# Chunk 0 of a three-stage kernel: first weights read as unsplit float32, one order for chunks 0 and 1, eight weight tiles split in the last chunk

## The chip, the core and the metric

The kernel runs on one core of one Trainium2 chip. The metric is device time in microseconds (us) of one execution. The kernel before took 981.0 us, the median of three runs (980.6 to 983.09). The engines are TensorE (PE, with its weight loads as PEld), VectorE (DVE), ScalarE (ACT), GpSimd (POOL) and the DMA queue of SyncE (SP).

## The reference

Three stages follow one another: a linear attention over 8 heads of width 64, a gated feed-forward layer (SwiGLU after an RMS norm), and a second feed-forward layer with a rational function in place of the gate.

```python
q_s = softmax(q, axis=-1); k_s = softmax(k, axis=2)
kv = np.einsum('bhsd,bhse->bhde', k_s, v)
x = np.einsum('bhsd,bhde->bhse', q_s, kv)            # as 2304 tokens x 512
xn = x / sqrt(mean(x * x) + 1e-06) * rms_g
y = (silu(xn @ w_gate) * (xn @ w_val)) @ w_out       # d_ff 1536
h = y @ w_in                                         # second layer, d_ff 2048
P = a[0] + a[1]*h + a[2]*h*h + a[3]*h*h*h
Q = 1.0 + abs(b[0])*abs(h) + abs(b[1])*h*h
out = (P / (Q + 1e-06)) @ w_out2
```

The weight matrices are float64. q, k, v and the output are float32.

## The kernel before, in words

The 2304 tokens are worked through in six chunks (c = 0 to 5) of T = 384 tokens. For each chunk the kernel makes the attention output x (four tiles of 128x384), its RMS norm, and then goes over f = 0 to 11, the twelve column blocks of the first layer: a projection g with the gate weights, a projection v with the value weights, the product u = silu(g)*v, and y += u times a tile of w_out. y goes to DRAM. When all six chunks are done, a last phase goes over the six chunks again with the sixteen blocks of the second layer (h, the rational function, o).

**Weights.** Each weight tile is 128x512 float64 in DRAM (512 KB). The first layer has 36 (numbered in order of need: g0, v0 are 0 and 1, then for each f the tiles g, v and the o of the block before), the second layer has 32. A tile is loaded raw and turned into float32 by four steps, `conv_exp` and `conv_low` (usually ACT), `conv_sign` and `conv_join` (DVE). Then it is split in two parts of the fast matmul format (fp32r): `conv_hi` (a rounding copy, ACT or DVE) and `conv_lo` (the rest, a subtraction on POOL). x and u are split in the same way, and a product is three fp32r matmuls (`mm3`, lines 649 to 651): high times high, high times low, low times high. One projection is 4 x 3 = 12 matmuls of 128x384.

**Order.** All engine queues are in program order. In chunk 0 the program order is the table `ORDER` (lines 23 to 44), a list of named events. `l7` loads tile 7, `ce7 cl7 cs7 cj7 ch7 co7` are its six steps, `g3 v3 s3 p3 ph3 pl3 y3` the steps of block 3 (projections, silu, product, high and low part of u, output projection), `a...` and `b...` are the attention of chunks 0 and 1, `arp arn arb` the RMS norm of chunk 0, `wN` are N dummy matmuls. Tables `LOW_ACT`, `HI_DVE` and `ALT` choose the engine of single steps. Chunk 0 thus holds the conversion and split of all 36 tiles, its own attention and that of chunk 1. Its first two blocks are projected before the norm is known (`g<-xr`), so g, u and x are multiplied by the norm afterwards (`scale_g`, `scale_u`, `x_mult`).

Chunks 1 to 5 run in a plain loop (line 1038, `u_step`). While chunks 1 to 4 are projected, `schedule(c + 1)` makes the next chunk's attention, and `stage` (line 247) loads, converts, splits and writes to DRAM ("parks") eight second-layer tiles per chunk, 32 in all; it uses the slots of tiles 0 to 3, which are therefore parked first and fetched again. Chunk 5 has no attention to make and only fetches parked tiles (`fetch_to`).

```python
 208         nc.gpsimd.tensor_tensor(
 209             out=t[:, 1, :], in0=tmps.pop(i).bitcast(F32), in1=t[:, 0, :], op=ALU.subtract
 210         )
1060                 tick = lambda part: None if last else stage(c, f, part)
```

Of the kernel before, what the change touches and what calls it, by code (L numbers as in the profile page):

```python
# [19 lines left out]
LOW_ACT = (0, 1, 3, 4, 5, 6, 7, 8, 9, 11, 13, 16, 17, 19, 20, 21, 22, 23, 24, 25, 27, 31, 32, 33)  # L20
HI_DVE = (0, 3, 11, 12, 13, 14, 15, 16, 18, 19, 20, 23, 24, 27, 28, 29, 33, 34)
ALT = ('bqd0', 'bqn0', 'bqn1', 'xm0', 'xl0', 'xm1', 'xl1', 'bxl0', 'bxl1', 'bxl3', 'gr0', 'pl0', 'pl1', 'pl2', 'pl5', 'pl9', 'pl11')
ORDER = """
w9 lk0 akm0 alq akt0 w4 lk1 akx0 lv0 lv1 aqm aks0 w1 akm1 akt1 w2 aqd1 akd0 akx1 aks1 w2 aqd0 ake0 akz0 aqe l0
akv0 w2 akd1 aqs lg ake1 akz1 ce0 l1 cl0 cl1 akn0 aqn0 cs0 ce1 akv1 axq0 cj0 axq1 aqn1 axq2 l2 akn1 cs1 cl2
axq3 blk axc0 l3 axx0 l4 axc1 axc2 axx1 axx2 ce2 ch0 axc3 axs0 axs1 bkz0 l5 co0 axh0 axs2 l6 axh1 l7 axx3 axh3
cj1 blv0 axs3 ch1 cs2 axh2 add1 bkm0 add2 axl0 cj2 ce3 l8 bkt0 add3 l9 bkx0 xw0 ce4 ch2 cl3 co1 axl1 ce5 axl3
bks0 arp axl2 xw1 g0 co2 bkd0 arn l10 cs3 cj3 xw2 ce6 v0 cl6 l11 ch3 l12 cl4 bke0 silu arb ars cl5 l13 cs4 g1
cj4 gm0 xw3 ch4 ce8 cs5 l14 co3 ce7 xm3 xm0 s0 xh0 cj5 gr0 xm2 p0 gm1 co4 cl7 xm1 ch5 cs6 ph0 xl0 l15 xh1 pl0
cj6 bkv0 co5 v1 l16 xl1 xh2 s1 xh3 cl9 y0 cs7 ce9 ch6 gr1 xl2 xl3 l17 cl8 cl10 l18 cl12 ce11 cj7 ch7 cs8 cl11  # L30
l19 p1 ph1 co6 bkz1 ce10 cs9 l20 co7 cj8 pl1 ch8 cj9 ce12 cs10 co8 ch9 cl13 bkn0 cj10 ch10 g2 v2 l21 cs11 ce14
cl14 co9 ce13 cj11 cs12 ch11 l22 co10 co11 s2 l23 cs14 y1 l24 cj12 g3 lc ch12 p2 cs13 cl16 ce17 cl17 l25 ph2
s3 cl15 ce16 ce19 v3 cj13 p3 g4 ce15 cl18 co12 ch13 cj14 v4 blq pl2 cl20 ph3 ch14 co13 s4 pl3 ce20 cs16 cs17
cs15 cj15 ch15 y2 ce18 l26 p4 co14 cj16 co15 ch16 l27 cl21 cj17 cs18 cl19 y3 ce22 g5 ce21 l28 cs19 l29 co16
cs20 ch17 cl22 ph4 ce23 cj18 const v5 ch18 ce26 co17 l30 cj19 s5 co18 cl23 ch19 cs22 cs21 cj20 g6 l31 bqm pl4
ch20 ce24 v6 co19 cl25 p5 cl26 ce25 cl27 co20 blr ph5 cl24 bqd1 y4 s6 cj21 bqd0 g7 cj22 ch21 co21 ch22 cs23
ce28 cs24 co22 p6 v7 l32 pl5 bqe cj23 ch23 ph6 co23 cj24 cl28 l33 pl6 ch24 s7 ce33 cl31 ce27 co24 y5 cs25 bkm1
cj25 g8 ce31 ce29 p7 ch25 bqs s8 cs26 y6 cl32 l34 blv1 ph7 cj26 co25 cl29 bqn0 ch26 bqn1 cs27 v8 pl7 p8 bkt1
ce32 cs32 cs28 bkx1 y7 cl34 bxq0 bks1 cj27 ce34 l35 ph8 bkd1 co26 ch27 cl30 ce30 g9 bxq1 cs29 bxc0 cj28 pl8
co27 cj29 bke1 cl33 bxx0 ch28 s9 ch29 bxc1 co28 bkv1 bxq2 bxs0 cs30 cj30 bxo0 ce35 bxx1 bkn1 ch30 bxo1 co29  # L40
bxc2 co30 cs31 v9 bxs1 cs33 bxq3 cj31 ch31 bxa1 bxx2 cl35 g10 p9 bxc3 ph9 bxs2 pl9 cj32 bxa2 bxx3 bxs3 cs34
co31 cs35 ch32 bxo2 v10 s10 bxa3 brp cj33 co32 bxo3 y8 p10 ch33 cj34 co33 brn ph10 g11 ch34 cj35 brb ch35 bxm0
bxm3 bxm1 s11 co34 v11 y9 pl10 bxl0 bxm2 p11 bxl3 bxl1 bxl2 y10 co35 ph11 pl11
# [4 lines left out]
def kernel(  # L48
# [66 lines left out]
    W1 = {}  # L115
    W2 = {}
# [5 lines left out]
    done = {"load": 0}  # L122
# [48 lines left out]
    def conv_low(i):  # L171
        w, r = words(i)
        if i in LOW_ACT:
            nc.scalar.activation(w[:, :, 0], w[:, :, 0], AF.Copy, scale=7.49 * 2.0 ** -32)
            return
        nc.vector.tensor_scalar(
            out=w[:, :, 0], in0=w[:, :, 0], scalar1=2.0 ** -29, scalar2=7.0,
            op0=ALU.mult, op1=ALU.min,
        )
# [82 lines left out]

    up = ctx.enter_context(tc.tile_pool(name="up", bufs=1))
# [232 lines left out]

    def rms_pe(c, rp):
# [64 lines left out]
    def x_scale(c, p, rp):  # L562
# [101 lines left out]
    def emit_y():  # L664
        c, f, uh, ul = pend_y.pop(0)
        w = W1["o", f]
        if f == 0:
            acc_y[c] = [pa.tile([P, 512], F32, tag=f"a{m}", name=f"y_{c}_{m}") for m in range(KD)]
        for m in range(KD):
            ws = slice(m * P, (m + 1) * P)  # L670
            mm3(acc_y[c][m][:, :T], w[:, 0, ws], w[:, 1, ws], uh, ul, f == 0, f == F1 - 1)
        if f == F1 - 1:
            t = big_tile(F32, ytag(c), f"y_{c}").rearrange("p (c n) -> p c n", n=T)
            for m, o in enumerate(acc_y.pop(c)):
                if c == NCH - 1 and m % 2:
# [116 lines left out]
    def o_pe(s):  # L792
# [5 lines left out]
        for t in range(TT):  # L798
# [25 lines left out]
    with tc.manual_schedule():  # L824

        k1 = bp.tile([P, 2, SC, D], F32, tag=big[3], name="k_0_1")
        v1 = bp.tile([P, 2, SC, VW], F32, tag=big[4], name="v_0_1")
# [3 lines left out]
        nc.vector.memset(cb[:, 1:2], -64.0 * LN2)  # L831
        for t in (vt0, v1):
# [3 lines left out]
        def warm(n):  # L836
            t = ps("warm")
# [12 lines left out]
        def engine(name, one, two):  # L850
            return two if name in ALT else one

        def bank(name, fn, pool=None, tag=None):
            def matmuls():
                t = ps(name) if pool is None else pool.tile([P, 512], F32, tag=tag, name=name)
# [22 lines left out]
        for n in range(1, 17):  # L878
# [233 lines left out]
```

## Time and profile before

| | before |
|---|---|
| runs | 980.6, 981.0, 983.09 us (median 981.0) |
| profiled execution, its own time | 980.75 us |
| its span, first to last instruction | 979.0 us |
| busy PE / PEld / DVE / ACT / POOL | 929.8 / 871.1 / 683.6 / 579.8 / 231.6 us |
| share of the span | 95 / 89 / 70 / 59 / 24 % |
| DMA moved | 108.92 MB, mean 111 GB/s |

The page gives busy time by engine, then the span in 40 slices of some 24.5 us with the busy share of each engine in tenths, and TensorE's granted clock in the same tenths. Matmuls overlap one another in the records, so the pace of TensorE is read from the distance between two starts, not from the length of one record.

### The profile page before, as it was taken

Reading aid. Unit: us, or ns where it says so; the run is one execution under the profiler, and the core shown is the slowest. Engines: PE = TensorE matmul, PEld = TensorE weight load, DVE = VectorE, ACT = ScalarE, POOL = GpSimd, SP = SyncE. Lnnn points to the kernel's source line nnn. Section 1 sums busy time; section 2 is a strip of 40 time slices with the busy share of each in tenths; the row PEclk is TensorE's granted clock in tenths of the full one; section 3 lists DMA queues with packets and bytes.
Section 4 is the critical chain, followed back from the end, with each engine's and each line's share of the span. In section 5 each row is a group of like instructions: output and inputs, shape, how many; then the busy total and the mean of one; then the engine's idle time right before and its main releaser. Section 6 shows DMA issues by size and latency. Waiting matters only on the chain.

```text
span 979.0 us, 14267 instructions
## 1 busy us (share of the span) xinstructions
PE 929.8 (95%) x5408; PEld 871.1 (89%) x5408; DVE 683.6 (70%) x1160; ACT 579.8 (59%) x1069; POOL 231.6 (24%) x208
## 2 busy tenths in 40 slices
PE   7777779999999999999999999999999999999998
PEld 6666679999989998999999999999999999999997
DVE  7999995667666657756730058877777777777776
ACT  3655653553354254336331268888788888878876
POOL 3855533000000000000002213423324224234222
PEclk8899989999999999999999999999999999999999
DMA  9996003346454726344448730010010010100000
GB/s 260 349 308 201 1 1 108 130 172 192 141 158 167 202 89 194 132 153 168 172 175 274 251 117 1 1 65 1 1 65 1 27 40 1 65 1 1 33 1 32
DMA packets 69588, 108.92 MB, mean 111 GB/s; under 512 B 22672, under 2 KB 49296, under 8 KB 69520
## 3 DMA queue, kind: packets, MB, share of 16 engines
q1 hardware_dynamic: 69520, 108.02, 34.6%
q8 instruction: 42, 0.69, 0.3%
q14 instruction: 26, 0.21, 0.1%
HBM read 79.70 MB, written 28.31 MB: 110 GB/s over the span
## 4 chain that ended last, share of the span: by engine, by line
PE 81%; DVE 11%; SPq 3%; DMA 2%; issue 2%; ACT 1%; DVEq 0%
PE h L651 7%; PE h L649 7%; PE o L804 7%; PE o L803 7%; PE h L650 7%; PE o L802 7%; PE vv L649 4%; PE vv L650 4%; PE vv L651 4%; PE y L651 4%; PE y L649 4%; PE y L650 4%; PE g L649 4%; PE g L651 4%; PE g L650 4%; DVE raw L183 3%
## 5 line engine op out<-in xcount | busy, mean ns | idle before, releaser
L790 POOL TENSOR_TENSOR gl<-t,gh 128x384 fp32r<-128x384 f32 x94 | 104.5, 1112 | 253.4 <-ACT gh L788 223.1
L651 PE MATMUL h<-y,wf 128*128 128x384 f32 x384 | 129.5, 337 | 0.0
L649 PE MATMUL h<-y,wf 128*128 128x384 f32 x384 | 129.3, 337 | 0.0
L650 PE MATMUL h<-y,wf 128*128 128x384 f32 x384 | 128.9, 336 | 0.0
L763 DVE SCALAR_TENSOR_TENSOR A<-S,absb,A 128x384 f32<-128x384 f32 x96 | 61.6, 642 | 92.9 <-ACT A L753 92.9
L687 ACT ACTIVATE uh<-u 128x384 fp32r<-128x384 f32 x72 | 37.8, 524 | 132.3 <-DVE u L696 113.2
L804 PE MATMUL o<-wf,gl 128*128 128x512 f32 x288 | 114.1, 396 | 0.0
L803 PE MATMUL o<-wf,gh 128*128 128x512 f32 x288 | 113.7, 395 | 0.0
L802 PE MATMUL o<-wf,gh 128*128 128x512 f32 x288 | 112.0, 389 | 0.0
L650 PE MATMUL y<-ul,w 128*128 128x384 f32 x288 | 98.0, 340 | 5.9 <-DVE ul L692 4.3
L649 PE MATMUL y<-uh,w 128*128 128x384 f32 x288 | 99.2, 344 | 4.5 <-ACT uh L687 4.5
L692 POOL TENSOR_TENSOR ul<-u,uh 128x384 fp32r<-128x384 f32 x18 | 19.2, 1068 | 329.5 <-ACT uh L687 329.4
L651 PE MATMUL y<-uh,w 128*128 128x384 f32 x288 | 96.9, 337 | 0.0
L649 PE MATMUL g<-x,w 128*128 128x384 f32 x248 | 86.6, 349 | 3.1 <-DVE w L200 3.1
L651 PE MATMUL g<-x,w 128*128 128x384 f32 x248 | 84.8, 342 | 3.4 <-POOL w L208 3.4
L696 DVE TENSOR_TENSOR u<-u,vv 128x384 f32<-128x384 f32 x60 | 33.0, 551 | 78.5 <-PE vv L651 78.5
L650 PE MATMUL g<-x,w 128*128 128x384 f32 x248 | 84.3, 340 | 0.0
L183 DVE TENSOR_SCALAR raw<-raw 128x512 uint16<-128x512 uint16 x68 | 63.5, 962 | 25.1 <-ACT raw L230 24.6
L703 ACT ACTIVATE u<-g 128x384 f32<-128x384 f32 x60 | 29.3, 488 | 82.1 <-PE g L651 82.1
L649 PEld LDWEIGHTS h<-y,wf 128*128 128x128 f32 x384 | 72.2, 188 | 4.1
L650 PEld LDWEIGHTS h<-y,wf 128*128 128x128 f32 x384 | 72.1, 188 | 4.0
L649 PE MATMUL vv<-x,w 128*128 128x384 f32 x208 | 70.5, 339 | 1.7 <-DVE u L696 1.7
(205 smaller groups left out, 2377.7 us busy)
## 6 DMA issues: line engine op xcount, KB each, us to landing
wf<-sd SPq DMA_DIRECT2D x48, 512.0 KB, 4.4
sd<-ws SPq DMA_DIRECT2D x32, 512.0 KB, 3.0
raw<-in_moe_w_out_dram SPq DMA_DIRECT2D x28, 512.0 KB, 5.0
raw<-in_moe_w_in_dram SPq DMA_DIRECT2D x16, 512.0 KB, 4.6
raw<-in_moe_w_gate_dram SPq DMA_DIRECT2D x12, 512.0 KB, 9.3
raw<-in_moe_w_val_dram SPq DMA_DIRECT2D x12, 512.0 KB, 10.4
k<-in_k_dram SPq DMA_DIRECT2D x8, 576.0 KB, 6.5
v<-in_v_dram SPq DMA_DIRECT2D x16, 288.0 KB, 6.9
```

Of the source, the lines that this page charges most:

```text
L183: nc.vector.tensor_scalar(out=h[:, :, 1], in0=h[:, :, 3], scalar1=0x8000, scalar2=None, op0=ALU.bitwise_and)
L649: nc.tensor.matmul(o, lhsT=lh, rhs=rh, start=start, stop=False)
L650: nc.tensor.matmul(o, lhsT=lh, rhs=rl, start=False, stop=False)
L651: nc.tensor.matmul(o, lhsT=ll, rhs=rh, start=False, stop=stop)
L687: nc.scalar.activation(uh, u, AF.Copy)
L696: nc.vector.tensor_tensor(out=u, in0=u, in1=vv[:, :T], op=ALU.mult)
L703: nc.scalar.activation(u, g[:, :T], AF.Silu)
L763: nc.vector.scalar_tensor_tensor(out=out, in0=in0, scalar=scalar, in1=in1, op0=op0, op1=op1)
L790: eng.tensor_tensor(out=r["gl"], in0=r["t"], in1=r["gh"], op=ALU.subtract)
L802: nc.tensor.matmul(o, lhsT=r["gh"][:, ts], rhs=w[:, 0], start=first, stop=False)
L803: nc.tensor.matmul(o, lhsT=r["gh"][:, ts], rhs=w[:, 1], start=False, stop=False)
L804: nc.tensor.matmul(o, lhsT=r["gl"][:, ts], rhs=w[:, 0], start=False, stop=last)
```

## The change

The diff touches four things.

1. Sixteen tiles (`WHOLE`: g and v of blocks 0 to 3, o of blocks 0 to 7) are joined into float32 tiles that stay in the slots of tiles 28 to 35, two to a slot. In chunk 0 `proj_whole` and `y_whole` multiply them unsplit, as plain float32, with unsplit x and u: one matmul in place of three. They are split as well, for the later chunks.
2. The early projection with x before the norm is gone; chunk 0 waits for its norm.
3. `ORDER` now covers chunks 0 and 1 and the attention of chunk 2 (`d...`); names carry the chunk (`g1_3`). The engine tables are new: 18 of the 36 `conv_lo` run on DVE, 7 of the `conv_low` and 3 of the `conv_hi`; in both chunks the low part of u is made on DVE. The loop starts at chunk 2.
4. Chunk 1 stages no second-layer tiles. The eight that it staged are loaded raw, converted and split in chunk 5 (`last_load`, `stage_last`, `last_split`), and are not parked.

```diff
-LOW_ACT = (0, 1, 3, 4, 5, 6, 7, 8, 9, 11, 13, 16, 17, 19, 20, 21, 22, 23, 24, 25, 27, 31, 32, 33)
+NF, NY = 4, 8
+WHOLE = (0, 1, 2, 3, 4, 5, 6, 7, 8, 9, 10, 13, 16, 19, 22, 25)
+LOW_DVE = (0, 4, 9, 14, 16, 24, 35)
+HI_DVE = (1, 3, 7)
+LO_POOL = (1, 6, 7, 8, 10, 12, 14, 15, 16, 17, 20, 22, 25, 28, 29, 32, 33, 34)
 ORDER = """
-w9 lk0 akm0 alq akt0 w4 lk1 akx0 lv0 lv1 aqm aks0 w1 akm1 akt1 w2 aqd1 akd0 akx1 aks1 w2 aqd0 ake0 akz0 aqe l0
+lg alk0 akz1 bkz1 akz0 bkz0 alq akm0 alk1 w28 akt0 alv1 aqm akx0 akm1 aqd1 w19 aks0 alv0 aqd0 akd0 w10 akt1
...
     def conv_join(i):
-        w, r = words(i)
-        tmps[i] = wp.tile([P, 512], U32, tag="tmp", name=f"tmp_{i}", bufs=2)
...
+        if i in WHOLE:
+            n, h = divmod(WHOLE.index(i), 2)
+            if n not in sh:
+                sh[n] = wp.tile([P, 1024], F32, tag=f"s{N1 - 1 - n}", name=f"whole_{n}")
+            tmps[i] = sh[n][:, 512 * h:512 * h + 512]
+            W1F[order[i][1:]] = tmps[i]
+        else:
+            tmps[i] = wp.tile([P, 512], F32, tag="tmp", name=f"tmp_{i}", bufs=2)
+        join(i, tmps[i].bitcast(U32))
...
     def conv_lo(i):
...
+        eng = nc.gpsimd if i in LO_POOL else nc.vector
+        eng.tensor_tensor(out=lo, in0=tmps.pop(i), in1=hi, op=ALU.subtract)
...
+    def last_load(n):
+        i = N1 + n
...
+    def last_split(n):
...
+        nc.scalar.activation(hi, tmp, AF.Copy)
+        nc.vector.tensor_tensor(out=lo, in0=tmp, in1=hi, op=ALU.subtract)
+
+    def stage_last(f, part):
+        n = f - 2
+        if part == 0 and 0 <= n - 1 < PARK:
+            last_split(n - 1)
+        if part == 1 and 0 <= n < PARK:
+            stage_words(1, n)
+        if part == 2 and 0 <= n < PARK:
+            stage_join(1, n)
...
+    def proj_whole(o, w, x):
+        for kk in range(KD):
+            ws = slice(kk * P, (kk + 1) * P)
+            nc.tensor.matmul(
+                o[:, :T], lhsT=w[:, ws], rhs=x[:, kk, :], start=(kk == 0), stop=(kk == KD - 1)
+            )
...
+    def y_whole(c, f, u):
+        for m, o in enumerate(acc_tiles(c, f)):
+            nc.tensor.matmul(
+                o[:, :T], lhsT=W1F["o", f][:, m * P:(m + 1) * P], rhs=u,
+                start=(f == 0), stop=(f == F1 - 1),
+            )
...
+        def project(c, which, f, t):
+            if c == 0 and f < NF:
+                proj_whole(t, W1F[which, f], st["xs", 0])
+            else:
+                proj(t, W1[which, f], c)
...
-        for c in range(1, NCH):
+        for c in range(2, NCH):
...
-                tick = lambda part: None if last else stage(c, f, part)
+                tick = lambda part: stage_last(f, part) if last else stage(c, f, part)
```

**What moves on DVE after the norm of chunk 0.** The rows below are DVE's queue from the end of the norm to the product of block 0 (`u_0...<-u_0...,v_...`). `raw` rows are conversions of a tile, `tmp` and `whole` are joins, `w` a high or low part, `xs` and `x_0` the normed x and its low part. Before:

```order
L183 TENSOR_SCALAR raw_295<-raw_295 128x512
L190 SCALAR_TENSOR_TENSOR tmp_412<-raw_295 128x512
L200 CAST w_432<-tmp_412 128x512
L183 TENSOR_SCALAR raw_299<-raw_299 128x512
L190 SCALAR_TENSOR_TENSOR tmp_460<-raw_299 128x512
L1004 TENSOR_TENSOR u_0_462<-g_380,rs_441 128x384
L183 TENSOR_SCALAR raw_316<-raw_316 128x512
L955 TENSOR_TENSOR xs_362<-xs_362,rs_441 128x384
L190 SCALAR_TENSOR_TENSOR tmp_479<-raw_316 128x512
L1007 TENSOR_TENSOR u_0_462<-u_0_462,rs_441 128x384
L955 TENSOR_TENSOR xs_362<-xs_362,rs_441 128x384
L1015 TENSOR_TENSOR u_0_462<-u_0_462,v_416 128x384
```

Changed:

```order
L659 TENSOR_TENSOR x_0_509<-xs_373,x_0_508 128x384
L201 SCALAR_TENSOR_TENSOR whole_379<-raw_462 128x512
L195 TENSOR_SCALAR raw_466<-raw_466 128x512
L195 TENSOR_SCALAR raw_377<-raw_377 128x512
L186 TENSOR_SCALAR raw_540<-raw_540 128x512
L195 TENSOR_SCALAR raw_423<-raw_423 128x512
L195 TENSOR_SCALAR raw_540<-raw_540 128x512
L201 SCALAR_TENSOR_TENSOR whole_358<-raw_423 128x512
L201 SCALAR_TENSOR_TENSOR whole_573<-raw_540 128x512
L1072 TENSOR_TENSOR u_0_560<-u_0_560,v_0_547 128x384
```

The scalings of u and the split of the first tiles are gone from this stretch; what stands between the norm and the first product is only conversions up to the join.

**What moves on TensorE at the first blocks.** `g_`, `v_` are the projections, `y_0` to `y_3` the four output tiles, `bkt` belongs to the attention of chunk 1. Before, the first output projection:

```order
L649 MATMUL y_0_560<-uh_0_492,w_465 128x384
L650 MATMUL y_0_560<-ul_0_498,w_465 128x384
L651 MATMUL y_0_560<-uh_0_492,w_465 128x384
L649 MATMUL y_1_561<-uh_0_492,w_465 128x384
L650 MATMUL y_1_561<-ul_0_498,w_465 128x384
```

Changed, from the first projection of chunk 0 on:

```order
L748 MATMUL g_0_532<-xs_373,whole_383 128x384 x4
L748 MATMUL v_0_547<-xs_373,whole_383 128x384 x4
L748 MATMUL g_1_575<-xs_373,whole_358 128x384 x4
L748 MATMUL v_1_592<-xs_373,whole_358 128x384 x4
L764 MATMUL y_0_607<-u_0_560,whole_573 128x384
L764 MATMUL y_1_608<-u_0_560,whole_573 128x384
L764 MATMUL y_2_609<-u_0_560,whole_573 128x384
L764 MATMUL y_3_610<-u_0_560,whole_573 128x384
L417 MATMUL bkt_628<-ident,m_0_586 128x128
L748 MATMUL g_2_633<-xs_373,whole_573 128x384 x4
```

Three matmuls have become one, which takes u itself and no longer its two parts.

**What moves on DVE at the end of chunk 0.** The rows end or begin around the product of block 11 (`u_11`). Before, the last rows of chunk 0 and the first of chunk 1:

```order
L200 CAST w_1403<-tmp_1371 128x512
L190 SCALAR_TENSOR_TENSOR tmp_1405<-raw_1151 128x512
L564 SCALAR_TENSOR_TENSOR xs_1248<-xs_1248,gk,brb 128x384 x4
L1015 TENSOR_TENSOR u_11_1419<-u_11_1419,v_1422 128x384
L573 TENSOR_TENSOR x_1_1413<-xs_1248,x_1_1412 128x384
L692 TENSOR_TENSOR ul_11_1471<-u_11_1419,uh_11_1469 128x384
L696 TENSOR_TENSOR u_0_1496<-u_0_1496,vv_0_1498 128x384
```

Changed (`w_861`, `w_388` are the low parts of tiles 2 and 3, `raw_1156`, `raw_1400` the conversions of tiles 35 and 34, `mq` and `q` the attention of chunk 2):

```order
L231 TENSOR_TENSOR w_861<-whole_358,w_861 128x512
L201 SCALAR_TENSOR_TENSOR tmp_1378<-raw_1055 128x512
L1072 TENSOR_TENSOR u_11_1376<-u_11_1376,v_11_1321 128x384
L231 TENSOR_TENSOR w_388<-whole_358,w_388 128x512
L231 TENSOR_TENSOR w_1383<-tmp_1378,w_1383 128x512
L477 TENSOR_REDUCE mq_1402<-q_1352 128x24
L802 TENSOR_TENSOR ul_10_1418<-u_10_1289,uh_10_1373 128x384
L485 TENSOR_TENSOR q_1352<-q_1352,mq_1402 128x768
L186 TENSOR_SCALAR raw_1156<-raw_1156 128x512
L802 TENSOR_TENSOR ul_11_1439<-u_11_1376,uh_11_1433 128x384
L195 TENSOR_SCALAR raw_1156<-raw_1156 128x512
L1072 TENSOR_TENSOR u_0_1441<-u_0_1441,v_0_1385 128x384
```

Before, every tile was converted when the last product of chunk 0 stood in the queue; now splits of early tiles and the conversion of tiles 34 and 35 stand behind it, among the first products of chunk 1.

## Rows read from the trace of the kernel before

**Rows 1.** The page: busy time, and 40 slices of the span (busy tenths).

```profile
PE 929.8 (95%) x5408; PEld 871.1 (89%) x5408; DVE 683.6 (70%) x1160; ACT 579.8 (59%) x1069; POOL 231.6 (24%) x208
PE   7777779999999999999999999999999999999998
```

**Rows 2.** Busy time by window: length, engines with instruction counts, clock, DMA share, GB/s.

```profile
33.00:158.60 125.60, 98.37 (x607) 89.51 (x608) 121.49 (x174) 67.77 (x120) 72.28 (x53) 0.92 0.49 152
158.60:238.70 80.10, 80.10 (x459) 78.60 (x458) 50.13 (x81) 36.57 (x67) 1.94 (x5) 1.00 0.45 152
520.00:540.00 20.00, 20.00 (x117) 20.00 (x116) 1.66 (x3) 3.96 (x8) 4.78 (x5) 1.00 0.79 252
```

**Rows 3.** TensorE in order of time: start, length, line, tiles, idle time before.

```profile
39.84 0.81 PE L553 MATMUL arb<-acc,ones 128*128 128x384 f32 x2
40.19 0.63 PE L649 MATMUL g<-xr,w 128*128 128x384 f32 x1
40.66 0.34 PE L650 MATMUL g<-xr,w 128*128 128x384 f32 x1
...
158.65 0.33 PE L649 MATMUL g<-x,w 128*128 128x384 f32 x1
158.82 0.33 PE L650 MATMUL g<-x,w 128*128 128x384 f32 x1
...
238.19 0.33 PE L649 MATMUL g<-x,wf 128*128 128x384 f32 x1
```

**Rows 4.** DVE in order of time, the same columns, up to the end of chunk 0.

```profile
23.34 0.76 DVE L183 TENSOR_SCALAR raw<-raw 128x512 uint16<-128x512 uint16 x1
23.87 0.47 DVE L176 TENSOR_SCALAR raw<-raw 128x512 uint32<-128x512 uint32 x1
...
24.58 0.69 DVE L190 SCALAR_TENSOR_TENSOR tmp<-raw 128x512 uint32<-128x512 uint32 x1
25.18 1.82 DVE L183 TENSOR_SCALAR raw<-raw 128x512 uint16<-128x512 uint16 x1
...
34.13 0.15 DVE L508 TENSOR_SCALAR rw<-arp 128x3 f32<-128x3 f32 x1
...
50.41 0.54 DVE L1004 TENSOR_TENSOR u<-g,rs 128x384 f32<-128x384 f32 x1
50.88 0.73 DVE L183 TENSOR_SCALAR raw<-raw 128x512 uint16<-128x512 uint16 x1
...
155.23 0.55 DVE L1015 TENSOR_TENSOR u<-u,v 128x384 f32<-128x384 f32 x1 [0.45 <-ACT u L1012]
```

**Rows 5.** Groups by line, operation and shape, 0 to 160 us: busy, mean ns, idle before.

```profile
L183 DVE TENSOR_SCALAR raw<-raw 128x512 uint16<-128x512 uint16 x36 | 39.5, 1150 | 0.1
L190 DVE SCALAR_TENSOR_TENSOR tmp<-raw 128x512 uint32<-128x512 uint32 x36 | 36.3, 1012 | 0.9 <-DVE raw L183 0.5
L345 DVE TENSOR_REDUCE m<-k 128x128 f32<-128x1152 f32 x4 | 8.6, 2155 | 3.6 <-DMA k<-in_k_dram 3.6
L428 DVE TENSOR_REDUCE sumq<-q 128x24 f32<-128x1536 f32 x2 | 3.5, 1752 | 0.0
L208 POOL TENSOR_TENSOR w<-tmp,w 128x512 fp32r<-128x512 f32 x36 | 55.0, 1531 | 52.7 <-DVE w L200 21.3 <-ACT w L202 20.2 <-issue 4.2
L385 PE MATMUL bkv<-v,k 64*64 64x65 f32 x144 | 4.6, 219 | 0.0
```

**Rows 6.** The same view from 160 us to the end.

```profile
L183 DVE TENSOR_SCALAR raw<-raw 128x512 uint16<-128x512 uint16 x32 | 24.0, 749 | 25.0 <-ACT raw L230 24.6
L190 DVE SCALAR_TENSOR_TENSOR tmp<-raw 128x512 uint32<-128x512 uint32 x32 | 22.2, 693 | 1.2
L242 DVE TENSOR_TENSOR ws<-tmp,ws 128x512 fp32r<-128x512 f32 x32 | 22.1, 691 | 20.2 <-ACT ws L241 20.2
```

**Rows 7.** What TensorE waited for, 33 to 158.6 us: total us, times, longest.

```profile
PE y L649 <- ACT uh L687: 4.5, 3, 3.8
PE y L650 <- DVE ul L692: 4.3, 4, 1.5
```

More of the change, by code (lines that the diff above doesn't have):

```diff
@@ L494, in x_out, with rms_pe_0 @@
             x_add(c, p, nc.vector)
+    def rms_pe_0(p, rp):
+        for t in range(TT):
+            nc.tensor.matmul(
+                rp[:, TT * p + t:TT * p + t + 1], lhsT=sh["sq_0"][:, p, t * P:(t + 1) * P],
+                rhs=ones[:, 0:1], start=True, stop=True,
+            )
     def rms_pe(c, rp):
@@ L848, in put, with bank @@
             ev[name] = lambda: fn(*args)
[L850 to L853 removed]
+        def bank(name, fn):
             def matmuls():
[L855 removed]
+                t = ps(name)
                 banks[name] = t
@@ new lines @@
+                put(f"{pre}xh{p}", x_high, c, p)
+                put(f"{pre}xl{p}", x_rest, c, p, nc.vector)
+            if c == 0:
+                bank("arp0", lambda t: rms_pe_0(0, t))
+                for p in range(1, NP):
+                    reader(f"arp{p}", "arp0", lambda t, p=p: rms_pe_0(p, t))
+                reader("arn", "arp0", rms_0)
+            else:
+                bank(f"{pre}rp", lambda t, c=c: rms_pe(c, t))
+                reader(f"{pre}rn", f"{pre}rp", lambda t, c=c: rms(c, t))
@@ new lines, with gate, mult_v @@
+            bank(f"{pre}rb", lambda t, c=c: spread_pe(c, t))
+        def gate(c, f):
+            if ("u", c, f) not in sh:
+                sh["u", c, f] = up.tile([P, T], F32, tag="u", name=f"u_{c}_{f}", bufs=2)
+            return sh["u", c, f]
+        def project(c, which, f, t):
+            if c == 0 and f < NF:
+                proj_whole(t, W1F[which, f], st["xs", 0])
+            else:
+                proj(t, W1[which, f], c)
+        def mult_v(c, f, v):
+            u = gate(c, f)
+            nc.vector.tensor_tensor(out=u, in0=u, in1=v[:, :T], op=ALU.mult)
@@ new lines, in high_u, with low_u, project_out, out_0 @@
+        def high_u(c, f):
+            sh["uh", c, f] = u_high(c, f, gate(c, f))
+        def low_u(c, f):
+            u_low(c, f, gate(c, f), sh["uh", c, f], nc.vector)
+        def project_out(c, f):
+            if c == 0 and f < NY:
+                y_whole(c, f, gate(c, f))
+            else:
+                emit_y(False)
+        def out_0(m):
+            if ("y", 0) not in st:
+                st["y", 0] = y_tile(0)
+            y_out(0, m, st["y", 0])
+        for c in range(2):
+            for f in range(F1):
+                for which in "gv":
+                    bank(f"{which}{c}_{f}", lambda t, c=c, which=which, f=f: project(c, which, f, t))
+                reader(f"s{c}_{f}", f"g{c}_{f}", lambda t, c=c, f=f: nc.scalar.activation(
+                    gate(c, f), t[:, :T], AF.Silu))
+                reader(f"p{c}_{f}", f"v{c}_{f}", lambda t, c=c, f=f: mult_v(c, f, t))
+                put(f"ph{c}_{f}", high_u, c, f)
+                put(f"pl{c}_{f}", low_u, c, f)
+                put(f"y{c}_{f}", project_out, c, f)
@@ L1033 @@
+        for m in range(KD):
+            put(f"ye0_{m}", out_0, m)
+        put("ly0", lambda: nc.sync.dma_start(out=y_d[0], in_=st["y", 0]))
         for name in ORDER.split():
             ev[name]()
-        for i, (which, f) in enumerate((("g", 0), ("v", 0), ("g", 1), ("v", 1))):
-            park(i, W1[which, f])
-        for c in range(1, NCH):
+        for c in range(2, NCH):
             last = c == NCH - 1
```

354 lines of the change are left out of this document (162 added, 192 removed).

## The prediction

> **What bounds the kernel now.** I read the page first. TensorE is busy 95% of the span and its slices stand at 9 tenths from the seventh on, at 7 before that [rows 1]: whatever can be won lies in the first 160 us. Then the windows [rows 2]. From 158.6 to 238.7 us, which is chunk 1, TensorE is busy 80.1 of 80.1 us at full clock. From 33 to 158.6 us, which is chunk 0 from its norm on, it is busy 98.4 of 125.6 us, while DVE is busy 121.5 of them. So DVE bounds chunk 0 and TensorE all the rest. The waits agree: TensorE waits there for the parts of u, which hang on DVE's product [rows 7].
>
> The first matmul of chunk 1 starts at 158.65 and that of chunk 2 at 238.19 [rows 3]; a chunk that keeps TensorE full takes 79.5 us. From 238.19 to the end of the profiled execution (its own time 980.75, 0.25 below the median, span 979.0) lie 742.6 us. The change leaves the loop of chunks 2 to 4 and the second layer as they are, so the forecast is T + 742.6, where T is when the first matmul of chunk 2 starts.
>
> **What TensorE has to do before T.** Two starts of fast-format matmuls of 128x384 lie 0.17 us apart [rows 3], so a triplet costs 0.52, one projection or output (4 triplets) 2.08. Plain float32 of the same shape is seen in the spread of the norm: line 553 is one matmul, recorded as two (`x2`). From its start at 39.84 to the start of the second fast one behind it, at 40.66, are 0.82 [rows 3]; less 0.17 for the fast one between, 0.645 are left for one plain matmul. Its bounds are 0.35 (the next start, 40.19) and 0.81 (its whole record); I take 0.645, because the fast matmul at 40.19 is the only one recorded with 0.63 and so can't have had TensorE to itself at once. Each of the 64 replaced triplets (8 projections and 8 outputs, 4 each) then costs 0.125 more: +8 us of TensorE.
>
> Chunk 0 after: 64 x 0.645 = 41.3; 16 split projections 33.3; 4 split outputs 8.3; and the attention of chunk 1. That of chunk 2, inside chunk 1, is what 79.5 leaves beside 36 x 2.08 = 74.9, so 4.6; chunk 1's has the k-v products on top, 4.6 [rows 5], and the k maxima, say 1.3. Together 93.4 us.
>
> **When it can start.** Before, DVE began the norm at 34.13 [rows 4]. The change takes out ahead of it a k maximum (2.16), a k subtraction (under 1.75) [rows 5] and the four rests of the early x (4 x 0.47), and puts in six conversion steps of 0.53 to 0.6: norm at about 31, give or take 3. From there to the spread matmul it took 5.7 (34.13 to 39.84) [rows 3, 4]; with four scalings of x at 0.47 the first projection starts at about 38. The early projection before the norm is lost; it won TensorE little, since the outputs behind it waited for DVE. If DVE never held it, T = 38 + 93.4 + 79.5 = 211.
>
> **What DVE has to do.** Undisturbed prices come from starts [rows 4]: sign 0.53, join 0.60 (24.58 to 25.18), a `conv_low` or a cast 0.355 (23.87 to 24.58, one of each), 384 columns 0.47 (50.41 to 50.88), small norm steps 0.2 (0.15 recorded and a gap). A split rest on DVE lasts as long as a join (691 against 693 ns) [rows 6], so 0.60. Wide steps: 2.16 for a k maximum, at most 1.75 for others [rows 5].
>
> Before, from the norm (34.13) to the end of the last product (155.78) [rows 4], DVE took 121.65 us for 33 signs 17.5, 33 joins 19.8, 28 lows and casts 9.9, 33 steps of 384 columns 15.5, seven wide 12.7, 37 small 7.4: together 82.8. The 38.8 missing lie beside 53 POOL instructions of 72.3 us [rows 2]: a sign takes 1150 ns there and 749 later, a join 1012 and 693 [rows 5, 6]; one sign beside POOL took 1.82 [rows 4]. So 0.73 us of DVE was lost per POOL instruction.
>
> After, from the norm to the product of block 6: 21 signs 11.1, 21 joins 12.6, 6 rests 3.6, 3 lows and casts 1.1, 15 of 384 columns 7.1, seven wide 13.1, 24 small 4.8: 53.3. Eleven POOL instructions stand beside it: 8.0 at 0.73. At worst each blocks its whole length, 1.53 [rows 5]: 16.8; at best nothing, 0. I take 8.0, since it is measured on this mixture. The product of block 6 then ends at 31 + 61.3 = 92.3.
>
> By then TensorE has 52.6 us of chunk 0 behind it if it was fed (8 plain projections 20.6, 6 split 12.5, 6 plain outputs 15.5, 4 of attention; it had 54 us), so DVE and TensorE run almost level here. Ahead lie 40.8 of chunk 0 and 79.5 of chunk 1: T = 92.3 + 120.3 = 212.6. Behind block 6 DVE falls back: the splits of tiles 2, 3, 34 and 35 stand behind the last product, but TensorE has four gate projections and three value projections of chunk 1 ahead of the outputs that need them, 7 x 2.08 = 14.6 us of cover.
>
> Two engines that run level wait for one another. Before, single waits for u were 1 to 1.5 us, the longest 3.8 [rows 7]. I add 4 us, three or four such waits: T = 216.7, and 742.6 + 216.7 = 959.3. A clock of 0.92, as in chunk 0 before [rows 2], on 93.4 us would cost 8: T = 219 by TensorE alone, 961.6, inside the same case.
>
> **What costs nothing, and its cover.** Eight tiles not staged in chunk 1: DVE (50.1 of 80.1 us) and ACT (36.6) had room there and TensorE was full [rows 2], so 0 gained. The same eight in chunk 5: chunk 1 carried the same steps and an attention on top without costing TensorE anything, and at 520 to 540 us DVE is busy 1.66 of 20, ACT 3.96 [rows 2], so 0. Were that cover gone (a split late for the second layer), one tile's chain of load and six steps would hold TensorE some microseconds once. A raw tile is as many bytes as a parked one, so the DMA share of 0.79 stays. The rests of u on DVE in chunk 1, twelve of 0.6 us, lie beside its slack.
>
> **The rivals.**
> *TensorE alone sets T* (POOL costs less than 0.73, no mutual waits): T = 211, 953.5 us, 948 to 956; 948 if the 64 plain matmuls are cheaper by 0.04 each (2.6) and the norm is 3 earlier. For: DVE leads by little. Chance 0.16.
>
> *POOL blocks DVE more.* At 1.53 an instruction the product of block 6 ends at 31 + 53.3 + 16.8 = 101.1, T = 221.4 + 4, 968. If instead all DVE work stretches as before (121.65/82.8 = 1.47), it ends at 109.4, T = 229.7, 972.3. Range 966 to 977. For: the sign of 1.82 us beside POOL. Against: 72.3 us of POOL cost DVE 38.8, half of it. Chance 0.2. The Trainium skill, page "SBUF — State Buffer", section "SBUF: two separate sides", says that the port pair which DVE and GpSimd share is an exclusive lock, held for the whole instruction, so that a DVE operation with two SBUF inputs fully blocks against a GpSimd operation that reads SBUF. By that rule the first of these two sums holds, 968; the trace of before shows 0.73 lost per POOL instruction of 1.36 us on average (72.3/53), about half of what the rule would take.
>
> *Slower: a lower clock in chunk 0.* If TensorE's granted clock falls to the 1.2 GHz level for so long that its mean from 38 us on is 0.7, 93.4 us become 133, T = 38 + 133 + 79.5 = 250.9, 993 us. It decides from a mean below 0.73 (T above 245). For: TensorE idles for pieces of the first 38 us, and plain float32 is new here. Against: it was granted 0.92 while it idled 22% of the time [rows 2]. Chance 0.05.
>
> *It does not do what it says: tiles come late.* The first three blocks' tiles must be loaded and joined sooner than before and the shared slots 28 to 35 are freed only when tiles 28 to 35 are wanted. If each of the last eight came 2.5 us late beyond the cover, the 20 us are gone: 978 to 984. Against: DMA is at half its share in chunk 0 [rows 2]. Chance 0.07.
>
> **How the numbers follow.** The forecast case, 956 to 966, has 0.52 and gives 959.5 us. The range takes in most of the first two rivals: 951 to 975 leaves out the slow clock, the late tiles and the tails of the rest, about 0.2. Less than 0.3% (2.9 us) can't be told from no change. Faster: 0.52 + 0.16 + 0.2 = 0.88; same: the late tiles, most of 0.07, say 0.06; slower: 0.06.
>
> **What would show it.** Right: first plain projection near 38 us; TensorE nearly full from there; first matmul of chunk 2 near 217 where 238.2 was; mean of the sign step nearer 749 than 1150 ns; chunk 5 still 20 of 20 busy. Four outputs in a row show the price of plain float32 at once. Wrong: TensorE idle for over 15 us between 40 and 217, with DVE's product as what it waits for (the POOL rival) or the rests of tiles 28 to 35 (late tiles); a clock under 0.85 there; idle TensorE in the last chunk or at the start of the second layer.

## The result and the profile after

The changed kernel takes 968.19 us (median of 4 runs, 967.86 to 970.56), the kernel before 981.65 beside it: a ratio of 0.9867, 95% interval 0.9846 to 0.9888, or 13.5 us less. Forecast were 959.5 us, in a range of 951 to 975. The profiled execution took 968.04 us at a span of 966.0.

The page, busy time by engine and the first two rows of slices:

```profile
PE 950.3 (98%) x5604; PEld 881.8 (91%) x5604; DVE 654.4 (68%) x1157; ACT 583.3 (60%) x1077; POOL 184.5 (19%) x173
PE   9998999999999999999999999999999999999998
```

Where six slices stood at 7 before [rows 1] now stand 9 and 8. But TensorE's busy time has risen, by more than the 8 us of plain float32: the profile counts dummy matmuls too, and there are more of them. The windows say where it is really at work (columns as in [rows 2]):

```profile
33.00:47.40 14.40, 14.38 (x123) 13.77 (x122) 7.97 (x26) 7.71 (x16) 2.50 (x2) 1.00 1.08 364
47.40:100.00 52.60, 48.35 (x247) 32.99 (x246) 50.31 (x74) 41.46 (x70) 13.76 (x9) 1.00 0.45 122
100.00:225.00 125.00, 125.00 (x759) 119.36 (x759) 70.92 (x136) 49.75 (x94) 19.53 (x17) 1.00 0.26 77
520.00:540.00 20.00, 20.00 (x117) 20.00 (x116) 9.02 (x12) 10.10 (x20) 7.03 (x7) 1.00 0.79 253
```

From 100 us to chunk 2 TensorE doesn't idle at all. From the first projection to 100 us it idles 4.2 us, and DVE is busy 50.3 of 52.6. The last row is chunk 5: DVE went from 1.66 to 9.02 of 20 us and ACT from 3.96 to 10.10 [rows 2], TensorE stayed at 20 of 20 and the DMA share at 0.79.

TensorE in order of time, up to the first projection, and the first matmul of chunk 2:

```profile
29.50 5.08 PE L948 MATMUL warm<-ident 128*128 128x128 f32 x44
34.41 1.40 PE L566 MATMUL arp<-ones,sq 128*128 128x1 f32 x12
35.67 0.89 PE L532 MATMUL axx<-qT,kv 128*128 128x384 f32 x2
36.40 1.57 PE L566 MATMUL arp<-ones,sq 128*128 128x1 f32 x12
37.83 5.60 PE L948 MATMUL warm<-ident 128*128 128x128 f32 x48
43.27 0.81 PE L633 MATMUL arb<-acc,ones 128*128 128x384 f32 x2
43.92 3.73 PE L948 MATMUL warm<-ident 128*128 128x128 f32 x32
47.49 0.81 PE L748 MATMUL g<-xs,whole 128*128 128x384 f32 x2
...
225.04 0.33 PE L735 MATMUL g<-x,w 128*128 128x384 f32 x1
```

Chunk 2 starts at 225.04 where it started at 238.19 [rows 3]: 13.15 us, all of the gain. Behind it lie 743.0 us, before 742.6. But the first projection starts at 47.49, not at 38. Ahead of, between and behind the parts of the norm on TensorE (`arp` sums the squares of x, `arb` spreads the result) three runs of dummy matmuls stand in the queue (`w22`, `w24`, `w16` of the order table). DVE's waits from 28 to 100 us (total, times, longest) show what that does:

```profile
DVE rw L584 <- PE arp L566: 3.5, 1, 3.5
DVE xs L644 <- PE arb L633: 2.6, 1, 2.6
DVE raw L195 <- ACT raw L181: 1.2, 2, 1.0
```

And TensorE's waits from 28 to 230 us, which together are the 4.2 us:

```profile
PE y L764 <- DVE u L1072: 2.6, 2, 1.6
PE bxq L513 <- POOL qn L505: 0.6, 1, 0.6
PE bkt L417 <- DVE m L411: 0.6, 1, 0.6
PE bkv L451 <- ACT k L442: 0.4, 1, 0.4
```

### The profile page after: what moved, and what is told of

Same layout as the page of the kernel before. It is cut to its first block, busy times and chain, and to the rows that moved or that the text cites. A ratio compares the mean times of both kernels' runs of the same rounds, so it can differ in the third digit from the quotient of the medians.

```text
span 966.0 us, 14546 instructions
## 1 busy us (share of the span) xinstructions
PE 950.3 (98%) x5604; PEld 881.8 (91%) x5604; DVE 654.4 (68%) x1157; ACT 583.3 (60%) x1077; POOL 184.5 (19%) x173
## 4 chain that ended last, share of the span: by engine, by line
PE 91%; SPq 3%; DMA 3%; DVE 3%; POOL 0%; ACT 0%; issue 0%; POOLq 0%
PE h L737 7%; PE h L735 7%; PE o L914 7%; PE o L913 7%; PE h L736 7%; PE o L912 7%; PE g L735 5%; PE g L737 5%; PE g L736 5%; PE y L735 4%; PE y L737 4%; PE y L736 4%; PE vv L735 3%; PE vv L736 3%; PE vv L737 3%; PE warm L948 2%
## 5 line engine op out<-in xcount | busy, mean ns | idle before, releaser
L737 PE MATMUL h<-y,wf 128*128 128x384 f32 x288 | 97.2, 337 | 0.0
L735 PE MATMUL h<-y,wf 128*128 128x384 f32 x288 | 97.0, 337 | 0.0
L736 PE MATMUL h<-y,wf 128*128 128x384 f32 x288 | 96.7, 336 | 0.0
L735 PE MATMUL y<-uh,w 128*128 128x384 f32 x256 | 87.8, 343 | 0.0
L736 PE MATMUL y<-ul,w 128*128 128x384 f32 x256 | 85.8, 335 | 0.0
L737 PE MATMUL y<-uh,w 128*128 128x384 f32 x256 | 85.7, 335 | 0.0
L914 PE MATMUL o<-wf,gl 128*128 128x512 f32 x216 | 85.5, 396 | 0.0
L913 PE MATMUL o<-wf,gh 128*128 128x512 f32 x216 | 85.3, 395 | 0.0
L912 PE MATMUL o<-wf,gh 128*128 128x512 f32 x216 | 84.0, 389 | 0.0
L898 ACT ACTIVATE gh<-t 128x384 fp32r<-128x384 f32 x96 | 50.4, 525 | 29.9 <-DVE t L873 29.7
L869 ACT ACTIVATE r<-A,cb 128x384 f32<-128x384 f32 x96 | 59.4, 619 | 10.1 <-DVE A L873 3.2
L862 ACT ACTIVATE S<-h 128x384 f32<-128x384 f32 x96 | 46.9, 488 | 29.7 <-PE h L737 27.8
L864 ACT ACTIVATE t<-h,na 128x384 f32<-128x384 f32 x96 | 64.6, 673 | 0.0
L870 ACT ACTIVATE r<-r,cb 128x384 f32<-128x384 f32 x96 | 59.3, 617 | 3.1
```

The lines of the kernel that those rows point to most:

```text
L735: nc.tensor.matmul(o, lhsT=lh, rhs=rh, start=start, stop=False)
L736: nc.tensor.matmul(o, lhsT=lh, rhs=rl, start=False, stop=False)
L737: nc.tensor.matmul(o, lhsT=ll, rhs=rh, start=False, stop=stop)
L864: nc.scalar.activation(r["t"], h, AF.Identity, scale=na[:, 3:4], bias=na[:, 2:3])
L869: nc.scalar.activation(r["r"], r["A"], AF.Ln, scale=LSC, bias=cb[:, 0:1])
L870: nc.scalar.activation(r["r"], r["r"], AF.Exp, scale=-1.0, bias=cb[:, 1:2])
```

## The experiments

The profile left two questions. Ratios below are against the kernel before, measured beside each run. Do the dummy runs hold the start, or would something else hold it as well? And how much of DVE's time does POOL take, since the rival by which POOL blocks for its whole length had named 968 us and 968.2 came?

**The dummy runs left out** (`no_warm3`) and **shortened** (`short_warm3`).

```diff
-... w22 arp0 ... w24 arb ... w16 g0_0
+... arp0 ... arb ... g0_0                  (left out)
+... w8 arp0 ... w13 arb ... w3 g0_0        (shortened)
```

> The changed kernel (968 us) without its three last runs of dummy matmuls ahead of the first projection (22, 24 and 16 of them). Theory, start time: the norm of chunk 0 and its first projection stand behind these runs in TensorE's queue, some 8 us; without them the first projection starts at 38 to 41 us, not 47.5, and the time is 960 to 964. Rival, DVE or the tiles set the first blocks anyway: the first projection is earlier, but TensorE then idles 8 us more before 95 us, time 966 to 969. Rival, clock: the granted clock falls in the gaps and the time is 968 or more.

> The same three runs shortened to 8, 13 and 3 dummy matmuls, so that they end about when their data is there. Start-time theory: 960 to 965, first projection at 39 to 42 us. DVE/tiles rival: 966 to 969. If the run without them lost its clock and this one does not, this one is the faster by 2 us or more; if the clock did not fall, they are within 2 us of each other.

Measured: 967.03 us (0.9845, 0.9827 to 0.9863) left out, 966.11 us (0.9843, 0.9822 to 0.9864) shortened; against the changed kernel's 968.19 these are 1.2 and 2.1 us less, under the 2.9 that a measurement tells apart. Both times lie in the range of the rival by which DVE or the tiles set the first blocks (966 to 969), above the 960 to 965 of the theory, and the two are 0.9 apart, not 2 or more; so the traces have to speak. Left out, TensorE's clock fell:

```profile
33.00:45.00 12.00, 7.40 (x20) 4.92 (x21) 8.91 (x28) 8.53 (x17) 2.50 (x2) 0.57 1.06 376
```

In this window it was granted 0.57, against 1.00 in the changed kernel; the first projection starts at 42.51, chunk 2 at 222.91. With the short runs the clock is 1.00 there, the first projection starts at 40.63 (6.9 earlier) and chunk 2 at 221.52 (3.5 earlier). So the dummy runs do hold the start, as the theory has it; but half of the 6.9 us is lost again, as the rival has it, in a place that the short version's waits of TensorE, 28 to 230 us, name in their first row:

```profile
PE g L748 <- DVE whole L201: 3.2, 1, 3.2
PE y L764 <- DVE u L1072: 2.7, 2, 1.6
PE bxq L513 <- POOL qn L505: 0.6, 1, 0.6
```

The gate projection of block 1 now waits 3.2 us for the join of its tile. TensorE idles 7.5 us in all, in place of 4.2. Both the start and the supply of the first blocks are limits, one close behind the other. The time went down less than the start of chunk 2 (2.0 against 3.5 us of span); the rest is under the last heading.

**Ten sign steps left out**, with the long and with the short dummy runs (`signs_out`, `signs_out_short`).

```diff
     def conv_sign(i):
+        if i in NO_SIGN:
+            return
```

> The changed kernel with ten sign steps of chunk 0 left out (tiles 2, 4, 5, 6, 7, 10, 14, 16, 17, 18; their weights then have wrong last bits or signs), all of which stand on DVE between the norm and the product of block 3. Theory, DVE bounds 45 to 95 us: DVE is 5 to 8 us shorter there, TensorE's 4.2 us of idle time nearly go, the first matmul of chunk 2 starts at 221 to 222 (225.0), time 964 to 965.5. Rival, ACT or the tiles' arrival bound it: 224 to 225, time 967 to 968.5.

> The same ten sign steps left out, and the three dummy runs shortened to 8, 13 and 3. Theory, the start and DVE are the two limits one behind the other: of the 7.9 us that TensorE idles with the short runs alone 5 or more go, the first matmul of chunk 2 starts at 215 to 218, time 959 to 962. Rival, with the earlier start the arrival of tiles bounds (DMA at its full share to 60 us): 219.5 or later, time 963 or more.

Measured: 968.55 us with chunk 2 at 224.15 for the first, a miss of the theory; the rival's numbers came (968.5 and 224 to 225). 961.90 us (0.9804, 0.9788 to 0.9820) with chunk 2 at 217.58 for the second, as the theory had it. DVE's waits in the first, 36 to 95 us, say what held it when it had less to do:

```profile
DVE rw L587 <- PE arp L569: 3.5, 1, 3.5
DVE mx L427 <- PE bkt L420: 2.9, 1, 2.9
DVE xs L647 <- PE arb L636: 2.6, 1, 2.6
DVE whole L204 <- ACT raw L182: 2.2, 1, 2.2
```

It ran into TensorE (`bkt` stands behind the plain matmuls in TensorE's queue) and into ACT's first conversion step. With the late start TensorE has 52.6 us to fill up to 100 and fills 48.4 of them: there were never more than 4.2 us to win from DVE. With the early start and the signs gone its idle time falls from 7.5 to 2.5 us. The early start alone gave 3.5 us at chunk 2, the missing signs alone 0.9, both together 7.5.

**All low parts on POOL, or none** (`LO_POOL = tuple(range(36))`, `LO_POOL = ()`; 18 in the change).

> The changed kernel with all 36 low parts of chunk 0 on POOL, not 18. Theory (0.73 us of DVE lost per POOL instruction, against 0.60 for one on DVE): 967 to 971. Rival, a POOL instruction blocks DVE for its whole length (1.4 to 1.5 us): DVE loses some 0.9 for each that is moved, about ten of them before TensorE has its backlog, 975 to 979.

> The changed kernel with all 36 low parts of chunk 0 on DVE, none on POOL. Theory (a POOL instruction costs DVE 0.73 us, one on DVE 0.60): no gain worth a measurement, 967 to 970. Rival, a POOL instruction blocks DVE for its whole length: DVE wins some 0.9 for each, and TensorE gets back most of its 4.2 us of idle time in chunk 0, 963 to 966.

Measured: 968.06 and 969.70 us, chunk 2 at 224.89 and 224.90. Neither moved it, as the theory had it. That alone could be because TensorE is nearly full; the price itself is in the groups of 0 to 160 us. None on POOL:

```profile
L195 DVE TENSOR_SCALAR raw<-raw 128x512 uint16<-128x512 uint16 x36 | 26.1, 761 | 1.8 <-ACT raw L181 1.7
L201 DVE SCALAR_TENSOR_TENSOR tmp<-raw 128x512 uint32<-128x512 uint32 x20 | 13.7, 697 | 0.0
L201 DVE SCALAR_TENSOR_TENSOR whole<-raw 128x512 uint32<-128x512 uint32 x16 | 10.8, 700 | 0.1
L1072 DVE TENSOR_TENSOR u<-u,v 128x384 f32<-128x384 f32 x14 | 7.8, 560 | 3.8 <-PE v L737 2.9 <-ACT x L651 0.7
```

All 36 on POOL:

```profile
L195 DVE TENSOR_SCALAR raw<-raw 128x512 uint16<-128x512 uint16 x36 | 32.5, 946 | 1.0 <-ACT raw L181 1.0
L201 DVE SCALAR_TENSOR_TENSOR tmp<-raw 128x512 uint32<-128x512 uint32 x20 | 18.7, 943 | 1.3 <-POOL w L231 1.2
L201 DVE SCALAR_TENSOR_TENSOR whole<-raw 128x512 uint32<-128x512 uint32 x16 | 14.9, 959 | 0.1
L1072 DVE TENSOR_TENSOR u<-u,v 128x384 f32<-128x384 f32 x14 | 7.7, 558 | 2.4 <-PE v L737 1.8 <-ACT x L651 0.5
```

A sign lasts 185 ns longer, a join some 250: 36 x 0.185 + 20 x 0.246 + 16 x 0.259 = 15.7 us for 36 POOL instructions, 0.44 each, in signs and joins alone. Other groups grow as well: the seven `conv_low` on DVE from 440 to 593 ns, the parts of x (L659, eight) from 726 to 836, small steps, most of them of the norm. With all groups of DVE but the low parts themselves it is 22.0 us, 0.61 for each POOL instruction: what one costs on DVE (0.60), and far from the 1.5 us for which it lasts. So it makes little difference to DVE where the low parts run (busy 129.5 and 131.0 of 160 us), which agrees with chunk 2 at the same place. The product `u`, whose second operand comes from PSUM, isn't longer at all (560, 558).

**The kernel before with the change's 18 low parts on DVE** (`before_lo18`). There DVE bounds 121 us, so a price shows in the time.

```diff
-        nc.gpsimd.tensor_tensor(
+        eng = nc.gpsimd if i in LO_POOL else nc.vector
+        eng.tensor_tensor(
```

> The kernel before with the low parts of the same 18 tiles as in the change on DVE, nothing else. DVE bounds its chunk 0, so the price shows fully. Theory: 18 x (0.60 - 0.73) = -2.3 us, 977 to 982. Rival, whole-length blocking: 18 x (0.60 - 1.53) = -17 us, 962 to 968. A third: on DVE each low part waits there for its high part on ACT, and the queue behind it stands, 984 or more.

Measured: 980.67 us, 0.9982 (0.9973 to 0.9992), 1.3 us under the 981.98 beside it; in its trace chunk 1 starts at 155.46 against 158.65 [rows 3], 3.2 us earlier. The theory's 2.3 lies between; the 17 us of whole-length blocking are not there. (Half of the 3.2 is lost again between 280 and 300 us, where the granted clock was 0.91; see the last heading.) The time is no clean price, since TensorE now waits for low parts that stand in DVE's queue; DVE's other groups of 0 to 160 us are shorter by some 0.9 us for each instruction moved (signs 1150 to 1014 ns, joins 1012 to 868).

**The cover of the last chunk, and chunk 1 without staging** (`last_fetched`, `before_no_stage1`). The first two lines are of `last_fetched`, whose chunk 5 then has nothing to convert or split either, the others of `before_no_stage1`.

```diff
-                last_load(done["load"] - N1)
+                fetch(done["load"])
...
+        if c == 1:
...
+            return
         if part == 0 and 0 <= f - 2 < PARK:
```

> The changed kernel, but the last chunk fetches eight parked tiles (of another number, so their values are not the right ones) in place of loading and splitting eight; everything before is the same. Theory: the splits in chunk 5 are covered, so 967 to 969. Rival: they hold TensorE or other steps there, so this is 965 or less.

> The kernel before without the staging in chunk 1: eight tiles fewer are loaded, converted, split and parked, and the last chunk fetches other parked tiles in their place, so their values are not the right ones. Theory: TensorE is full in chunk 1 anyway, 980 to 983. Rival: staging costs something in chunk 1 or at its start, 977 or less.

Measured: 967.96 us beside the change's 968.19, and 982.83 us with a ratio of 1.0005 (0.9995 to 1.0015). Both came as the theory had it: the splits in chunk 5 cost nothing in the changed kernel, and chunk 1 without staging brings nothing in the kernel before.

**Towards a better version.** In both kernels TensorE stops twice for 2.1 us in the loop, for DVE's normalization of q. It was moved forward, on top of the short dummy runs (`short_warm3_qn`) and in the kernel before (`before_qn`):

```diff
-        put(15, lambda: q_norm(c, eng))
+        put(13, lambda: q_norm(c, eng))
```

> The short dummy runs, and in the attention of chunks 3 to 5 DVE's normalization of q two places earlier, right behind its sums. Theory: TensorE's two stops of 2.1 us each for it go, and with them the stretch at half clock behind the second: 4.2 us less than the short runs alone (966.1), 960 to 962.5. Rival: what is pushed back on DVE by 1.75 us (the reciprocals of the k-v products, a conversion) holds TensorE in its place: 964 to 967.

> The kernel before with the same move of q's normalization. The two stops of 2.1 us are in its trace as well, so they have nothing to do with the change: 976 to 979 (981.9). Rival as for the short runs: 980 or more.

Measured: 967.99 and 984.20 us. The second is worse (1.0022, 1.0012 to 1.0033), as the rival had it; the first, 1.9 us above the short runs alone, is 1 us above its rival's range too, and by itself under what a measurement tells apart. TensorE's waits of the first from 222 us on:

```profile
PE y L735 <- ACT uh L797: 3.2, 2, 1.6
PE vv L735 <- DVE u L806: 1.7, 2, 0.8
PE vv L735 <- DVE kv L471: 0.9, 2, 0.4
PE kt L417 <- DVE m L411: 0.4, 2, 0.2
```

The stops for `qn` (4.3 us in two) are gone, and the product of u, pushed back on DVE, comes late: its high part holds TensorE twice for 1.6 us, the products with the reciprocals twice for 0.4. In both kernels TensorE falls back by 0.6 to 0.7 us at each of the two places. The last attempt placed chunk 1's attention later in the order, again with short dummy runs (`late_b60`; loads stayed where they were, so part of its v is overwritten before it is read).

> The three short dummy runs, and the steps of the attention of chunk 1 placed later in the order (60 places later at its first k maximum, fading to none at its norm), nothing left out: its q maximum and a subtraction, 4 us of DVE, move behind the product of block 3. Theory, the start and DVE are the two limits one behind the other: as with the ten signs left out, the first matmul of chunk 2 starts at 217.5 to 219.5 in place of 221.5, time 961.5 to 964. Rival, DVE's total up to the k-v products is what counts: the wait only moves to the k-v products of chunk 1 or to the first projections of chunk 1, 221 or later, time 966 or more.

Measured: 971.11 us (0.9888, 0.9869 to 0.9907), chunk 2 at 228.31. The rival held; TensorE's waits, 28 us to the end:

```profile
PE bkt L416 <- DVE m L410: 3.0, 1, 3.0
PE y L763 <- DVE u L1071: 2.8, 2, 1.4
PE g L747 <- DVE whole L200: 2.6, 1, 2.6
PE v L734 <- DVE k L436: 2.4, 1, 2.4
```

The waits of 3.0 and 2.4 us are new. `bkt` stands in TensorE's queue ahead of a projection and waits for its k maximum; the projection `v` waits until DVE's subtraction has read `bks`, 1.3 us long and late on DVE, and with it the queue behind it. That is 3.3 us more idle time than with the short runs alone (10.8 and 7.5), about half of what chunk 2 is later (6.8). The rest fits the clock: TensorE was granted 0.94 from 47.4 to 100 us, 1.00 in the other. No version here that does all the work beats the changed kernel by more than a measurement can tell; the short dummy runs (966.11) come nearest.

## Why the prediction was right in the whole and wrong in one step

The time lay in the range and on the right side, and the main mechanism fits the one that was named: chunk 0 was bound by DVE, the plain float32 takes splits out of DVE's way, and TensorE fills. No run has the new order without the plain float32 tiles, so how the 13.15 us divide between the two is not shown. But 968 us is the figure of the POOL rival, and that rival's mechanism is not what happened. Step by step:

- **TensorE's work up to chunk 2.** Forecast 93.4 + 79.5 = 172.9 us. Measured 225.04 - 47.49 - 4.2 idle = 173.35. A plain projection lasts 2.58 (47.49 to 50.07, the start of the next), so 0.645 for a matmul, the price worked out from one instance before. (The fast matmul at 40.19 was not the only one of that trace recorded with 0.63, another is at 152.10; the price does not hang on it.)
- **When it can start: this step failed.** The prediction said that the norm begins at about 31 and the first projection at 38, "give or take 3". They began at 38.0 and 47.5, and nearly the whole miss is here. It counted only the work that the change takes from DVE's queue ahead of the norm. The norm hangs on TensorE as well, and in TensorE's queue the change puts 62 dummy matmuls (`w22`, `w24`, `w16`) around its parts. Shortening them gave back 6.9 of the 9.5 us. With them short the norm still starts at 36.0, not 31, and `arp` holds it only 0.6 us there: DVE's own queue ahead of it ends at 35.4 (in the changed kernel at 34.5; this execution's first dummy run took 0.9 us longer). DVE's work there was counted rightly, its waits were not. They lie in the attention of chunk 0. DVE's waits for `aks` and `akt` ahead of the norm, two rows of the changed kernel and two of the kernel before:

```profile
DVE k L437 <- PE aks L432: 3.4, 2, 2.1
DVE mx L424 <- PE akt L417: 1.4, 2, 1.1
...
DVE k L371 <- PE aks L366: 1.0, 1, 1.0
DVE mx L358 <- PE akt L351: 0.4, 1, 0.4
```

  These are 3.4 us more, and k and q from DRAM held DVE 0.9 us longer; without the 4.3 us the queue would end at some 30.2, near the forecast's 31. `akt` and `aks` stand behind dummy matmuls too: the order's first five runs have 76 of them (`w28` to `w9`), where the kernel before has 20 up to the same place, and TensorE goes over to the waiting step only when the run ends:

```profile
16.80 2.50 PE L948 MATMUL warm<-ident 128*128 128x128 f32 x20
19.14 0.39 PE L432 MATMUL aks<-ident,mb 128*128 128x128 f32 x2
```

  No run shortens these five, so what that would give, and what it would cost in clock, is not shown.
- **DVE's work.** It was sized about rightly. From the norm at 38.0 to the end of block 6's product at 103.8 are 65.8 us, 6.1 of them waits: 59.7 of work, where 61.3 were forecast. The mean sign step is 851 ns, nearer 749 than 1150. But the product (with that of block 5) had itself waited for TensorE, as its row in DVE's order of time says:

```profile
102.82 1.02 DVE L1072 TENSOR_TENSOR u<-u,v 128x384 f32<-128x384 f32 x2 [1.49 <-PE v L737]
```

  DVE was busy 50.3 of the 52.6 us up to 100, TensorE 48.4: level, as forecast. With the late start TensorE is the nearer limit: ten signs less on DVE brought 0.9 us, the earlier start 3.5.
- **Mutual waits.** 4 us were put in, 4.2 measured, but that is partly luck: they were put in for a start at 38, and with the start at 40.6 they were 7.5.
- **POOL.** 0.73 us lost per instruction lies between what the runs show for all groups of DVE, 0.61 in the changed order and some 0.9 in the kernel before, where the 18 moved ones gave 1.3 to 3.2 us and 2.3 was worked out. The Trainium skill, page "SBUF — State Buffer", section "SBUF: two separate sides", says that the loser of the shared port pair fully blocks for the other's whole instruction. That a DVE operation which takes an operand from PSUM isn't held agrees with that section (557 to 560 ns in all three kernels). A whole 1.5 us for each POOL subtraction, as the rival took it, did not come: the runs show 0.61 on the mean.
- **Costs of nothing.** Chunk 5's splits and chunk 1's missing staging (this in the kernel before) are at zero, as forecast, by two runs of their own.
- **Clock and late tiles.** Neither came: the granted clock was 1.00 in every stretch shown up to chunk 2. (The mark of 0.73 in the clock's rival doesn't follow from its sum: the time passes 981 us at T = 238.4, which is a mean of 0.77.)

So, followed along TensorE, the sum was short by 9.5 at the start, by 0.4 each in TensorE's work and behind chunk 2, and by 0.2 in the waits; it was too long by 1.7, since it went by DVE's path (212.6), not TensorE's (211). Together 8.8; the distance from 959.3 to 968.04 is 8.7. Along DVE, the path that the prediction took, it is the same step: 7.0 late at the norm, 2.1 more in waits (6.1, not 4), 1.6 less in work, 0.9 more from block 6's product to chunk 2 and 0.4 behind it.

## What to carry to other kernels

Before a stage is dated, follow its first instruction's inputs through every queue that they pass, TensorE's own among them: dummy matmuls that keep the clock up are work in an in-order queue, and behind them stands whatever needs TensorE next. Size them to end when the data comes; without the last three runs the clock fell to 0.57 ahead of the first projection, and chunk 2 came 1.4 us later than with short ones. When a time agrees with a rival, look whether its mechanism is in the trace before believing it. And where two limits lie a few us apart, taking away one shows little; only both together showed 7.5 us here.

## What the runs showed that was not expected

**A stop of 2.1 us sometimes costs 1.6 more.** Several executions lose some 1.5 us behind one of the two stops for `qn` in the loop. TensorE in the version with short dummy runs, behind its second stop for `qn`:

```profile
357.54 0.52 PE L513 MATMUL xq<-ident,qn 128*128 128x128 f32 x3 [2.14 <-DVE qn L505]
...
358.68 0.52 PE L736 MATMUL vv<-x,w 128*128 128x384 f32 x1
359.00 0.52 PE L737 MATMUL vv<-x,w 128*128 128x384 f32 x1
...
361.88 0.35 PE L737 MATMUL y<-uh,w 128*128 128x384 f32 x1
```

In the changed kernel, at the same place of the program:

```profile
361.07 0.52 PE L513 MATMUL xq<-ident,qn 128*128 128x128 f32 x3 [2.11 <-DVE qn L505]
...
362.49 0.33 PE L735 MATMUL vv<-x,w 128*128 128x384 f32 x1
362.66 0.33 PE L736 MATMUL vv<-x,w 128*128 128x384 f32 x1
```

After the same stop the starts lie 0.32 us apart in the one, from 358.7 to 361.9, and 0.17 in the other: TensorE ran at its lower level (1.2 GHz) for some 3 us, or did not. That is why the short version's 3.5 us at chunk 2 are 2.0 at the end, and why `lo_all_dve`, with chunk 2 at the same place as `lo_all_pool`, ends 1.6 later: it was granted 0.91 from 260 to 280 us, the other 1.00, both with the same stop. The profiled executions of `no_warm3` and `signs_out` show the same 0.91 there. What decides between the two was not settled.

**Not every DVE operation feels POOL.** Signs and joins grow by a quarter to over a third when all low parts are on POOL, k maxima (2169 to 2182 ns) and products with a PSUM operand by next to nothing, so a price per POOL instruction holds only for the mixture on which it was measured.
